# Attention and two feed-forward blocks on one core: GpSimd's arithmetic moved to VectorE, the first load split, the first scores turned round

## The chip, the cores and the metric

The kernel runs on one core of one Trainium2 chip. The metric is the device time of one execution in microseconds, the median over several runs. The engines are named as the profile names them: PE (TensorE, products and transposes), DVE (VectorE), ACT (ScalarE), POOL (GpSimd) and SP (SyncE, which here only issues DMAs).

## What is computed

The reference, cut to what matters; all of it is float32:

```python
scores = scale * np.matmul(q, k.transpose(0, 1, 3, 2))   # 2 batches, 12 heads, 448 x 64
scores = np.where(mask, -1000000000.0, scores)            # causal
scores = scores - np.max(scores, axis=-1, keepdims=True)
attn = np.exp(scores)
attn = attn / (np.sum(attn, axis=-1, keepdims=True) + 1e-09)
x = np.matmul(attn, v)                                    # -> 896 x 768
h = (x @ w1) * (x @ w2) @ w3 @ w_out                      # 768 -> 1024 -> 1024 -> 768
r = np.maximum(h @ w_in2, 0.0)                            # 768 -> 2048
out = (r * r) @ w_out2                                    # 2048 -> 768
```

## The kernel before

Everything is one stream of operations. A class `Program` (L28) collects them with what they read and write; `order` (L60) then lays them out by a list scheduler of its own, with a cost on each engine that may do the operation, and the kernel issues them in that order (L1287 to L1289), so the order on every engine is fixed when the program is built. Each operation is *due* when the PE step that needs it would start. An operation with two engines in its cost table goes where the planner finds it sooner: ACT or DVE for some copies, DVE or POOL for the scaling of the softmax (L688) and for subtractions whose operands all lie in SBUF (L446, L1029). POOL takes one of these if it would be done before DVE could begin it, or if it is due more than `SPARE` = 2500 ns later (L104). The flag `port` makes the planner keep a flagged operation of DVE or POOL from starting before the last flagged one of either has ended (L91).

The work runs in stages. *Attention* (to about 158 us in the profile): twelve pairs of heads. For a pair p, `load_pair` (L603) brings q and k, `scores` (L620) makes the scores of four row blocks of 112 (widths 448, 336, 224 and 112, because of the causal mask; `BLOCKS` at L600 gives the order, 448 first, and puts the last two in one PSUM bank), `minimum` (L660) adds the mask and takes each row's extreme on DVE, `softmax` (L666) takes the exponential with its sums on ACT, the reciprocal on DVE and the scaling of `p` on DVE or POOL (L689), `transposes` (L693) turns the scaled blocks on PE into `pp`, which ACT copies to `pt`, and `attend` (L714) makes `x`. The scores of pair p stand ahead of the transposes of pair p-1. After the scores of the second pair `warm` (L755) puts 36 transposes of the identity on PE. Between them PE multiplies `w3` and `w_out` (`w_half`, L558; tiles `w` and `wraw`), so that one weight replaces the two; their raw words go through `float32` (L482: L487 on ACT, L491 and L495 on DVE).

*First block* (158 to 320 us): products by Strassen's scheme in seven products (`product`, L1061; `h_step`, L1116). Every operand is split into a high part (rounded, ACT L440) and a low part (the rest, a DVE subtraction, L433), and three products of parts stand for one; `parts_of` (L442) adds these two operations. The weights' parts lie in `ring`, their sums in `xs`, other rows in `fs`. POOL adds the sums of the replaced weight by DMA (L821). *Second block* (from 320 us): the same for `w_in2`, then `g_out` (L1004), `need_block` (L1020) and `o_step` (L1208), whose sums go into `g` by DVE additions from PSUM (`g<-bank,g`).

One helper makes all subtractions, so they all stand at L433, all matrix products at L176, all copies at L440; the tiles tell them apart. What the change touches, with its callers:

Of the kernel before, what the change touches and what calls it, by code (L numbers as in the profile page):

```python
# [8 lines left out]
F32 = mybir.dt.float32  # L9
# [7 lines left out]
class Op:  # L17
# [4 lines left out]
    def __init__(self, place, engines, run, after, behind, port):  # L22
        self.place, self.engines, self.run, self.port = place, engines, run, port
        self.after, self.behind = after, behind
        self.due = self.start = self.end = None


class Program:  # L28
# [4 lines left out]
    SPARE = 2500  # L33
# [4 lines left out]
    def add(self, engines, run, reads=(), writes=(), port=False, after=(), behind=(), turn=None):  # L38
# [11 lines left out]
        op = Op(len(self.ops), engines, run, list(after), [o for o in behind if o not in after], port)  # L50
# [9 lines left out]
    def order(self):  # L60
# [18 lines left out]
        port, at_step = 0, 0  # L79
        avail = dict.fromkeys(ready, 0)  # L80
        while ready:
            best = None
            for e in clock:
# [6 lines left out]
                def begin(o):  # L90
                    held = port if e in "PV" and o.port else 0  # L91
                    return max(clock[e], avail[o], held)
# [5 lines left out]
                if e in "AP":  # L98
# [15 lines left out]
            if e in "PV" and o.port:  # L114
                port = t0 + gap
# [13 lines left out]
def attention_moe_moe2(ctx: ExitStack, tc: tile.TileContext, qk, v, w1, w2, w3, w_out, w_in2, w_out2, out):  # L129
# [21 lines left out]
    WARM = 36  # L151
# [186 lines left out]
    prog = Program({"S": 700})  # L338
    pools = {}
    engine_of = {"A": nc.scalar, "V": nc.vector, "P": nc.gpsimd}  # L340
# [8 lines left out]

    def pool(width):  # L350
        gap = 110 + 2.28 * width
        return {"P": (gap, gap + 30)}
# [89 lines left out]
    def parts_of(hi, lo, x, width, src, his, los, psum=False, any_engine=False, of=None):  # L442
# [39 lines left out]
    def float32(key, words, width, y, names):  # L482
# [16 lines left out]
        prog.add(dve(width, fast=True), lower, [low], [low], port=True)  # L499
        prog.add(dve(width), join, [low, *names], names, port=True)  # L500
# [14 lines left out]
    def w_row(key):  # L515
# [26 lines left out]
        prog.add(dve(width), tt(lo, y, lambda: hi_of(key).bitcast(F32), ALU.subtract), src + his, los, port=True)  # L542
# [60 lines left out]
    def load_pair(p):  # L603
# [4 lines left out]
        prog.add({"S": (1350, 3300)}, run, [], [("qk", p % 3)], turn="qk")  # L608
# [10 lines left out]

    def scores(p):  # L620
# [6 lines left out]
        for g in BLOCKS:  # L627
            for j in range(2):
                at[j, g] = turn("a", 6)
        for g in BLOCKS:  # L630
            o = 0
            for i in g:
                w = (i + 1) * CP

                def run(e, g=g, i=i, o=o, w=w):
                    if g == BLOCKS[0]:
# [8 lines left out]
                opened = [place_p(p, j, i2) for j in range(2) for i2 in range(NCH)] if g == BLOCKS[0] else []  # L645
                prog.add({"T": (1.856 * w, 1.856 * w + 250)}, run, [("qk", p % 3)],
                         [("a", at[j, g]) for j in range(2)] + opened)
                o += w
        for j in range(2):
            for g in BLOCKS:  # L650
# [15 lines left out]
    def softmax(p, j):  # L666
# [17 lines left out]
        for g in BLOCKS:  # L684
            for i in g:
                w = (i + 1) * CP
                on_v, on_p = 70 + 0.67 * w, 265 + 2.5 * w
                prog.add({"V": (on_v, on_v + 85), "P": (on_p, on_p + 30)},  # L688
                         lambda e, i=i: engine_of[e].tensor_scalar(  # L689
# [64 lines left out]

    def warm():  # L755
# [14 lines left out]

    for p in range(NP_ALL + 1):
# [64 lines left out]
    for k in range(KH):  # L836
        i, b = slot_in("T2", k), slot_in("B21", k)
        prog.add(dve(S), tt(fs_at(i), fs_at(b), fs_at(i), ALU.subtract), [("fs", i), ("fs", b)], [("fs", i)], port=True)
# [14 lines left out]
    def half_sum(out, x, z, what):  # L853
# [5 lines left out]
        prog.add(dve(HN), tt(half(out), half(x), half(z), what), [xs_half(*x), xs_half(*z)], [xs_half(*out)], port=True)  # L859
# [32 lines left out]
    def need_unit(u):  # L892
# [25 lines left out]
        else:  # L918
# [5 lines left out]
                 src + [("ring", i, "h") for i in slots], [("ring", i, "l") for i in slots], port=True)  # L924
# [19 lines left out]
    def ab_out(nm, m, b, n, i_bank):  # L944
# [12 lines left out]
        else:  # L957
            prog.add(dve(S), negated(row, fs_at(n), fs_at(a), ALU.mult), [("fs", n), ("fs", a)], names, port=True)
# [21 lines left out]
    def ab_sums(d):  # L980

        (r0, n0), (r1, n1), (r2, n2), (r3, n3) = (ab_row(d, i) for i in range(4))
        prog.add(dve(S), tt(r0, r0, r1, ALU.subtract), n0 + n1, n0, port=True)
        prog.add(dve(S), tt(r1, r3, r1, ALU.subtract), n1 + n3, n1, port=True)

        def t2():
            t = take_fs()
            prog.add(dve(S), negated(fs_at(t), r3, r0, ALU.subtract), n3 + n0, [("fs", t)], port=True)
            block_parts("ab", "T2", d, fs_at(t), ("fs", t))
            prog.add(dve(S), negated(r2, r2, fs_at(t), ALU.subtract), [*n2, ("fs", t)], n2, port=True)  # L990
# [13 lines left out]
    def g_out(nm, m, b, n, i):  # L1004
# [10 lines left out]
        parts_of(*part, lambda: fs[:, n, BN:], REST, ("fs", n), his, los, any_engine=True)  # L1015
# [4 lines left out]
    def need_block(g, n, d):  # L1020
# [7 lines left out]
        def sub(out, x, y):  # L1028
            prog.add(dve(BN) | pool(BN), tt(fs_at(out, BN), fs_at(x, BN), fs_at(y, BN), ALU.subtract),  # L1029
                     [("fs", x), ("fs", y)], [("fs", out)], port=True)  # L1030
# [6 lines left out]
        elif n == "7":  # L1037
# [3 lines left out]
                 his, los, any_engine=True)  # L1041
# [101 lines left out]
    def h_out(n, k, st, i):  # L1143
        o, src = bank_at(i), ("bank", i)

        def block(name, at):
            block_parts("h", name, k, fs_at(at), ("fs", at), any_engine=True)
# [4 lines left out]
        def sub(out, x, y):  # L1152
            prog.add(dve(S), tt(fs_at(out), fs_at(x), fs_at(y), ALU.subtract), [("fs", x), ("fs", y)], [("fs", out)],
# [184 lines left out]
```

## Time and profile before

| | us |
|---|---|
| median of 3 runs | 534.0 (533.85 to 537.04) |
| the profiled execution | 534.52 |
| its span on the core | 532.7 |
| PE busy | 519.2 |
| DVE busy | 492.3 |
| ACT busy | 383.9 |
| POOL busy | 103.2 |

The span runs from the core's first instruction to its last; the rest of the execution's time lies around it. Busy time is what an engine's instructions cover; those of DVE that follow each other overlap by some 0.08 us, so a row's mean is longer than the step from one to the next. PE's products are pipelined and their ends are modelled, so a busy PE may still be waiting a little.

### The profile page before, as it was taken

Reading aid. Unit: us, or ns where it says so; the run is one execution under the profiler, and the core shown is the slowest. Engines: PE = TensorE matmul, PEld = TensorE weight load, DVE = VectorE, ACT = ScalarE, POOL = GpSimd, SP = SyncE. Lnnn points to the kernel's source line nnn. Section 1 sums busy time; section 2 is a strip of 40 time slices with the busy share of each in tenths; the row PEclk is TensorE's granted clock in tenths of the full one; section 3 lists DMA queues with packets and bytes.
Section 4 is the critical chain, followed back from the end, with each engine's and each line's share of the span. In section 5 each row is a group of like instructions: output and inputs, shape, how many; then the busy total and the mean of one; then the engine's idle time right before and its main releaser. Section 6 shows DMA issues by size and latency. Waiting matters only on the chain.

```text
span 532.7 us, 8568 instructions
## 1 busy us (share of the span) xinstructions
PE 519.2 (97%) x2905; PEld 460.8 (86%) x2905; DVE 492.3 (92%) x1093; ACT 383.9 (72%) x890; POOL 103.2 (19%) x84
## 2 busy tenths in 40 slices
PE   7899999999999999999999999999999999999996
PEld 4658878888879999999999999999999989998985
DVE  5999898898999999997975899999999999999996
ACT  6998887777869565648475577986896489649950
POOL 2222211122110010221100034010115021505050
PEclk9999999999999999999999999999999999999999
DMA  8956554452642469999652402405430454035114
GB/s 317 322 166 220 169 180 148 147 170 61 249 156 83 177 184 252 260 254 248 153 163 93 172 0 73 165 1 201 155 120 0 148 178 150 0 132 175 51 59 149
DMA packets 26572, 81.30 MB, mean 153 GB/s; under 512 B 2400, under 2 KB 13408, under 8 KB 26528
## 3 DMA queue, kind: packets, MB, share of 16 engines
q1 hardware_dynamic: 22752, 75.24, 41.4%
q0 software_dynamic: 3776, 5.51, 6.4%
q8 instruction: 23, 0.38, 0.3%
q14 instruction: 21, 0.17, 0.1%
HBM read 74.84 MB, written 14.55 MB: 168 GB/s over the span
## 4 chain that ended last, share of the span: by engine, by line
PE 54%; DVE 21%; ACT 7%; DMA 2%; issue 2%; DVEq 0%
PE bank L176 43%; DVE g L433 6%; DVE ring L433 5%; PE w L176 5%; DVE xs L433 2%; DVE xs L495 2%; PE pp L704 2%; PE x L176 2%; DVE fs L433 2%; PE s L176 2%; ACT ring L440 1%; DMA raw_w<-in_w 1%; DMA raw_wout<-in_w_out 1%; ACT fs L1010 1%; ACT fs L1011 1%
## 5 line engine op out<-in xcount | busy, mean ns | idle before, releaser
L440 ACT CAST ring<-xs 128x384 fp32r<-128x384 f32 (+1 forms) x194 | 102.3, 542 | 59.2 <-DVE xs L433 21.4
L176 PE MATMUL bank<-xT,ring 128*128 128x448 f32 x630 | 132.2, 366 | 0.0
L433 DVE TENSOR_TENSOR ring<-xs,ring 128x384 fp32r<-128x384 f32 (+1 forms) x194 | 118.9, 631 | 12.2 <-ACT ring L440 12.0
L176 PEld LDWEIGHTS bank<-xT,ring 128*128 128x128 f32 x630 | 117.8, 188 | 9.6 <-ACT bank L440 0.5
L176 PE MATMUL bank<-ring,g 128*128 128x384 f32 x600 | 107.7, 337 | 3.0 <-DVE ring L433 2.0
L176 PEld LDWEIGHTS bank<-ring,g 128*128 128x128 f32 x600 | 103.8, 188 | 6.5 <-DVE ring L433 3.3
L176 PE MATMUL bank<-xB,ring 128*128 128x448 f32 x489 | 103.5, 367 | 0.7 <-ACT ring L440 0.4
L176 PEld LDWEIGHTS bank<-xB,ring 128*128 128x128 f32 x489 | 91.3, 188 | 10.0 <-ACT ring L440 1.4
L433 POOL TENSOR_TENSOR g<-fs,g 128x384 fp32r<-128x384 f32 (+1 forms) x24 | 37.2, 1562 | 127.7 <-ACT g L440 112.5
L672 ACT ACTIVATE p<-p,st 112x448 f32<-112x448 f32 (+3 forms) x96 | 49.9, 533 | 12.1 <-DVE st L662 12.1
L689 POOL TENSOR_SCALAR p<-p,st 112x224 f32<-112x224 f32 (+3 forms) x27 | 33.5, 1244 | 114.3 <-DVE st L681 62.4
L433 DVE TENSOR_TENSOR xs<-xs 128x384 f32<-128x384 f32 x96 | 54.4, 581 | 0.1
L662 DVE CUSTOM_DVE_ANT_0 p<-s,mask 112x224 f32<-112x224 f32 (+3 forms) x96 | 36.7, 440 | 6.4 <-PE s L176 6.3
L440 ACT CAST g<-fs 128x384 fp32r<-128x384 f32 (+1 forms) x88 | 34.4, 413 | 5.2 <-DVE fs L433 4.9
L176 PE MATMUL w<-hl_wout,w 128*128 128x384 f32 x192 | 36.2, 340 | 0.3 <-DVE wraw L433 0.2
L487 ACT ACTIVATE xs<-raw_w 128x768 f32<-128x768 f32 (+1 forms) x30 | 24.3, 814 | 14.7 <-DVE w L433 6.5
L176 PEld LDWEIGHTS w<-hl_wout,w 128*128 128x128 f32 x192 | 32.9, 188 | 1.9 <-issue 0.9
L821 POOL DMA_DIRECT2D s_dram<-w_dram x12 | 13.9, 1184 | 99.6 <-DMA s_dram<-w_dram 99.6
L176 PE MATMUL s<-qk 64*112 64x448 f32 (+3 forms) x192 | 28.2, 439 | 3.9 <-DMA qk<-in_qk 3.9
L433 DVE TENSOR_TENSOR g<-bank,g 128x384 f32<-128x384 f32 x60 | 30.1, 544 | 1.6 <-PE bank L176 1.6
L440 ACT COPY fs<-bank 128x448 f32<-128x448 f32 x49 | 25.8, 527 | 7.6 <-PE bank L176 7.6
L176 PE MATMUL bank<-ab,ring 128*128 128x448 f32 x144 | 29.5, 365 | 0.0
(82 smaller groups left out, 746.7 us busy)
## 6 DMA issues: line engine op xcount, KB each, us to landing
raw_wout<-in_w_out SPq DMA_DIRECT2D x24, 768.0 KB, 4.5
raw_w<-in_w SPq DMA_DIRECT2D x16, 768.0 KB, 4.5
raw_win<-in_w_in SPq DMA_DIRECT2D x16, 768.0 KB, 4.5
raw_w<-in_w SPq DMA_DIRECT2D x16, 512.0 KB, 4.1
qk<-in_qk SPq DMA_DIRECT2D x12, 448.0 KB, 5.7
s_dram<-w_dram POOLq DMA_DIRECT2D x8, 576.0 KB, 9.8
w_dram<-wraw SPq DMA_DIRECT2D x8, 384.0 KB, 2.9
s_dram<-w_dram SPq DMA_DIRECT2D x4, 768.0 KB, 7.1
```

The source lines that it names most:

```text
L176: return nc.tensor.matmul(o, l, r, start=start, stop=stop, **more)
L433: return lambda e: engine_of[e].tensor_tensor(out(), x(), y(), op=what)
L440: return lambda e: engine_of[e].copy(out(), x()) if e == "A" else engine_of[e].tensor_copy(out(), x())
L487: nc.scalar.activation(y(), raws[key][:, :, 1].bitcast(F32), AF.Prelu, scale=2.0 ** -112, alpha=-2.0 ** 32)
L495: nc.vector.scalar_tensor_tensor(yi, yi, 3, raws.pop(key)[:, :, 0], op0=ALU.logical_shift_left, op1=ALU.bitwise_or)
L662: prog.add({"V": (gap, gap + 160)}, lambda e: nc.vector.tensor_tensor_reduce(block(p, j, i), s_t[p, j, g][:CP, o:o + w], mask[:, S - w:], ...
L672: prog.add({"A": (gap, gap + 100)}, lambda e, i=i: nc.scalar.activation(block(p, j, i), block(p, j, i), AF.Exp, bias=st_t[p][:, 0, j, i:i ...
L689: lambda e, i=i: engine_of[e].tensor_scalar(block(p, j, i), block(p, j, i), st_t[p][:, 3, j, i:i + 1], None, ALU.mult),
L704: nc.tensor.transpose(x[0][:CP, o * CP:(o + 1) * CP], block(p, j, i)[:, c * CP:(c + 1) * CP], ident[:CP, :CP])
L821: prog.add({"P": (900, 5000)}, lambda e, x=x, n0=n0, n1=n1: nc.gpsimd.dma_start(out=s_dram[d][:, n0:n1], in_=spread(x, n1 - n0), accum_op= ...
L1010: prog.add(act(S, src[0] == "bank"), lambda e: nc.scalar.activation(r(), x(), AF.Relu), [src], [("fs", n)])
L1011: prog.add(act(S), lambda e: nc.scalar.activation(r(), r(), AF.Square), [("fs", n)], [("fs", n)])
```

## The change

Five edits, of which the first goes through the whole kernel.

1. POOL is left out of every cost table, and with it the `port` rule and `SPARE`: the 60 computing instructions that POOL had (27 scalings of `p`; 18 of `g` with 384 columns and 6 with 64; 8 of `fs`; 5 of `x` parts with 448 columns; in all of these but the scalings a subtraction) stand on DVE. POOL keeps the constants, the identity, the mask and the 12 DMAs that add. One copy to `wraw` goes from ACT to DVE by the planner's choice.
2. The first q and k tile comes in two DMAs of 224 columns each of q and k; the first two row blocks wait for the first only.
3. The first pair's blocks are taken from the narrowest on.
4. Ahead of them, five products of a 112x112 block of zeros, which DVE clears.
5. `warm` has 16 transposes instead of 36, and the planner prices the first pair's scores higher.

The diff, cut to its core:

```diff
-                if e in "AP":
+                if e == "A":
...
-                        return t0 + o.engines[e][0] < on_v or e == "P" and o.due > t0 + self.SPARE
+                        return t0 + o.engines[e][0] < on_v
...
-    WARM = 36
+    WARM = 16
+    WARM_UP = 5
...
-    prog = Program({"S": 700})
+    prog = Program({"S": 700, "V": 700})
...
-        engines = dve(width) | (pool(width) if any_engine else {})
-        prog.add(engines, tt(lo, x, lambda: hi().bitcast(F32), ALU.subtract), src + his, los, port=not psum)
+        prog.add(dve(width), tt(lo, x, lambda: hi().bitcast(F32), ALU.subtract), src + his, los)
...
+        def halves_of(n):
+            def run(e):
+                if n == 0:
+                    qk_t[p] = attq.tile([P, 2, S], F32, tag="qk", name=f"qk{p}", bufs=3)
+                own = slice(n * 2 * CP, (n + 1) * 2 * CP)
+                nc.sync.dma_start(
+                    out=qk_t[p][:, :, own], in_=qk[p].rearrange("p (i s) -> p i s", i=2)[:, :, own])
+
+            return run
+
+        if p == 0:
+            for n in range(2):
+                prog.add({"S": (675, 2400)}, halves_of(n), [], [("qk", p % 3, n)], turn="qk")
+            return
...
+        blocks = BLOCKS[::-1] if p == 0 else BLOCKS
...
-                prog.add({"T": (1.856 * w, 1.856 * w + 250)}, run, [("qk", p % 3)],
+                prog.add({"T": (cold(p, i) * w, cold(p, i) * w + 250)}, run, [("qk", p % 3, n) for n in range(1 + (i > 1))],
...
-                on_v, on_p = 70 + 0.67 * w, 265 + 2.5 * w
-                prog.add({"V": (on_v, on_v + 85), "P": (on_p, on_p + 30)},
+                on_v = 70 + 0.67 * w
+                prog.add({"V": (on_v, on_v + 85)},
...
+    def warm_up():
+        place = turn("w", 2)
+        prog.add({"V": (200, 300)}, lambda e: nc.vector.memset(xs[:CP, 0, :CP], 0.0), [], [("xs", 0, 0)])
+
+        def run(e):
+            t, x = ps_w.tile([P, HN], F32, tag="w", name="warm_up"), xs[:CP, 0, :CP]
+            for _ in range(WARM_UP):
+                mm(t[:CP, :CP], x, x, True, True)
...
-            prog.add(dve(BN) | pool(BN), tt(fs_at(out, BN), fs_at(x, BN), fs_at(y, BN), ALU.subtract),
-                     [("fs", x), ("fs", y)], [("fs", out)], port=True)
+            prog.add(dve(BN), tt(fs_at(out, BN), fs_at(x, BN), fs_at(y, BN), ALU.subtract),
+                     [("fs", x), ("fs", y)], [("fs", out)])
```

How the instructions stand. The last number of a name is that of its buffer. In a score's name the first number is the head of the pair and the second the block (3 is the one of 448 columns; 0 stands for the bank that blocks 0 and 1 share). PE at the start of the program, before:

```order
L176 MATMUL s_0_3_123<-qk_114 112x448
L176 MATMUL s_1_3_125<-qk_114 112x448
L176 MATMUL s_0_2_129<-qk_114 112x336
L176 MATMUL s_1_2_131<-qk_114 112x336
L176 MATMUL s_0_0_134<-qk_114 112x112
L176 MATMUL s_1_0_136<-qk_114 112x112
L176 MATMUL s_0_0_134<-qk_114 112x224
L176 MATMUL s_1_0_136<-qk_114 112x224
```

and after the change:

```order
L173 MATMUL warm_up<-xs 112x112 x5
L173 MATMUL s_0_0_129<-qk_115 112x112
L173 MATMUL s_1_0_131<-qk_115 112x112
L173 MATMUL s_0_0_129<-qk_115 112x224
L173 MATMUL s_1_0_131<-qk_115 112x224
L173 MATMUL s_0_2_139<-qk_115 112x336
L173 MATMUL s_1_2_141<-qk_115 112x336
L173 MATMUL s_0_3_147<-qk_115 112x448
L173 MATMUL s_1_3_149<-qk_115 112x448
```

The products of zeros stand first, and the order of the blocks is turned round.

DVE where the first pair's softmax ends (`p_121` and `p_122` are its two heads, `st_120` its sums; L662 is the minimum of the second pair), before:

```order
L662 ISA p_146,st_145<-s_0_2_156,mask 112x336
L662 ISA st_145 112x1
L689 TENSOR_SCALAR p_121<-p_121,st_120 112x448
L689 TENSOR_SCALAR p_121<-p_121,st_120 112x336
L689 TENSOR_SCALAR p_121<-p_121,st_120 112x112
L680 TENSOR_SCALAR st_120<-st_120 112x4
L681 RECIPROCAL st_120<-st_120 112x4
L662 ISA p_147,st_145<-s_1_2_158,mask 112x336
L662 ISA st_145 112x1
```

with POOL's first scalings, which stand behind its mask:

```order
L332 AFFINE_SELECT mask<-mask 112x448
L689 TENSOR_SCALAR p_121<-p_121,st_120 112x224
L689 TENSOR_SCALAR p_122<-p_122,st_120 112x224
L689 TENSOR_SCALAR p_146<-p_146,st_145 112x224
L689 TENSOR_SCALAR p_146<-p_146,st_145 112x112
```

DVE after the change, where `p_127` and `p_128` are the first pair's heads and L699 is the scaling:

```order
L699 TENSOR_SCALAR p_127<-p_127,st_126 112x448
L699 TENSOR_SCALAR p_127<-p_127,st_126 112x336
L699 TENSOR_SCALAR p_127<-p_127,st_126 112x224
L699 TENSOR_SCALAR p_127<-p_127,st_126 112x112
L690 TENSOR_SCALAR st_126<-st_126 112x4
L691 RECIPROCAL st_126<-st_126 112x4
L672 ISA p_160,st_158<-s_1_2_170,mask 112x336
L672 ISA st_158 112x1
L699 TENSOR_SCALAR p_128<-p_128,st_126 112x448
L699 TENSOR_SCALAR p_128<-p_128,st_126 112x336
L699 TENSOR_SCALAR p_128<-p_128,st_126 112x224
L699 TENSOR_SCALAR p_128<-p_128,st_126 112x112
```

POOL's two scalings of 224 columns now stand among DVE's, one for each head.

The end of the second block, POOL before (the last of its instructions):

```order
L433 TENSOR_TENSOR g_3578<-fs,g_3578 128x384
L433 TENSOR_TENSOR fs<-fs 128x384
L433 TENSOR_TENSOR g_3406<-fs,g_3406 128x384
L433 TENSOR_TENSOR g_3578<-fs,g_3578 128x384 x2
L433 TENSOR_TENSOR g_3406<-fs,g_3406 128x384 x2
L433 TENSOR_TENSOR fs<-fs 128x384 x2
L433 TENSOR_TENSOR g_3371<-fs,g_3371 128x384
```

DVE after the change, in the same part of the program (L426 is the helper's subtraction or addition):

```order
L426 TENSOR_TENSOR ring<-xs,ring 128x384
L426 TENSOR_TENSOR g_3569<-fs,g_3569 128x384
L426 TENSOR_TENSOR g_3537<-bank_1948,g_3537 128x384
L426 TENSOR_TENSOR g_3537<-bank_2186,g_3537 128x384
L426 TENSOR_TENSOR ring<-xs,ring 128x384
L426 TENSOR_TENSOR g_3569<-fs,g_3569 128x384
L426 TENSOR_TENSOR xs<-xs 128x384
L426 TENSOR_TENSOR fs<-fs 128x384
L426 TENSOR_TENSOR xs<-xs 128x384
L426 TENSOR_TENSOR g_3537<-bank_1946,g_3537 128x384
L426 TENSOR_TENSOR ring<-xs,ring 128x384
L426 TENSOR_TENSOR g_3284<-fs,g_3284 128x384
```

The `fs<-fs` and `g<-fs,g` subtractions stand between the parts of the weights (`ring<-xs,ring`) and the additions from PSUM (`g<-bank,g`), all on one engine.

## Rows read from the trace of the kernel before

**Rows 1.** The page, busy time of each engine, its share of the span and instructions.
```profile
PE 519.2 (97%) x2905; PEld 460.8 (86%) x2905; DVE 492.3 (92%) x1093; ACT 383.9 (72%) x890; POOL 103.2 (19%) x84
```

**Rows 2.** Windows by stage: length, then PE, PEld, DVE, ACT, POOL, clock, DMA.
```profile
0.00:27.00 27.00, 21.76 (x149) 15.37 (x150) 20.50 (x78) 20.72 (x57) 6.40 (x13) 1.00 0.90 319
27.00:160.00 133.00, 132.25 (x889) 104.87 (x888) 123.49 (x367) 105.56 (x292) 28.74 (x22) 1.00 0.50 167
160.00:320.00 160.00, 160.00 (x791) 148.14 (x791) 142.59 (x252) 102.92 (x197) 19.63 (x17) 1.00 0.61 169
320.00:388.00 68.00, 67.97 (x358) 64.46 (x357) 66.14 (x130) 55.92 (x125) 12.12 (x8) 1.00 0.35 120
388.00:524.00 136.00, 132.30 (x699) 123.31 (x698) 135.63 (x263) 98.28 (x223) 36.30 (x24) 1.00 0.29 98
```

**Rows 3.** Waits of PE, 388 to 524 us: total, times, longest.
```profile
PE bank L176 <- DVE ring L433: 2.0, 3, 0.7
```

**Rows 4.** Chain that ended last, in order of time, one piece: start, length.
```profile
398.83 1.87 DVE g L433 x4
```

**Rows 5.** Timeline of PE, 0 to 28 us: start, length, instruction, idle before.
```profile
3.90 6.69 PE L176 MATMUL s<-qk 64*112 64x448 f32 x32 [3.90 <-DMA qk<-in_qk]
10.53 3.66 PE L761 MATMUL warm<-ident 112*112 112x112 f32 x36
14.03 2.08 PE L704 MATMUL pp<-ident,p 112*112 112x112 f32 x20
16.04 2.22 PE L176 MATMUL x<-pt,v 112*64 112x448 f32 x16
18.18 2.15 PE L176 MATMUL s<-qk 64*112 64x448 f32 x16
20.66 2.85 PE L176 MATMUL w<-xs,w 128*128 128x384 f32 x8 [0.33 <-DVE w L495]
...
25.83 1.29 PE L704 MATMUL pp<-ident,p 112*112 112x112 f32 x10 [0.92 <-DVE p L689]
```

**Rows 6.** POOL by line and shape, 388 to 524 us: busy, mean ns, idle.
```profile
L433 POOL TENSOR_TENSOR g<-fs,g 128x384 fp32r<-128x384 f32 x15 | 23.2, 1559 | 63.0 <-ACT g L440 47.8 <-DVE g L433 15.2
L433 POOL TENSOR_TENSOR fs<-fs 128x384 f32<-128x384 f32 x7 | 10.1, 1446 | 18.4 <-DVE fs L433 18.4
```

**Rows 7.** Timeline of DVE around 499 us.
```profile
499.10 0.22 DVE L433 TENSOR_TENSOR g<-fs,g 128x64 fp32r<-128x64 f32 x1
499.23 0.55 DVE L433 TENSOR_TENSOR xs<-xs 128x384 f32<-128x384 f32 x1
```

**Rows 8.** DVE by line and shape, 388 to 524 us.
```profile
L433 DVE TENSOR_TENSOR ring<-xs,ring 128x384 fp32r<-128x384 f32 x74 | 44.4, 624 | 0.0
L433 DVE TENSOR_TENSOR xs<-xs 128x384 f32<-128x384 f32 x39 | 24.1, 630 | 0.0
L433 DVE TENSOR_TENSOR g<-bank,g 128x384 f32<-128x384 f32 x48 | 24.0, 543 | 0.0
...
L433 DVE TENSOR_TENSOR fs<-fs 128x384 f32<-128x384 f32 x17 | 10.9, 644 | 0.0
...
L433 DVE TENSOR_TENSOR g<-fs,g 128x64 fp32r<-128x64 f32 x19 | 4.8, 261 | 0.2
```

**Rows 9.** DVE by line and shape, 160 to 240 us.
```profile
L433 DVE TENSOR_TENSOR ring<-xs,ring 128x384 fp32r<-128x384 f32 x42 | 22.6, 548 | 0.9 <-ACT ring L440 0.9
```

**Rows 10.** Timeline of DVE, around 520 us.
```profile
520.10 1.08 DVE L433 TENSOR_TENSOR ring<-xs,ring 128x384 fp32r<-128x384 f32 x1
```

**Rows 11.** Timeline of all engines, 0 to 16 us.
```profile
0.74 0.86 SPq L606 DMA_DIRECT2D qk<-in_qk  x2
...
5.89 0.62 DVE L662 CUSTOM_DVE_ANT_0 p<-s,mask 112x448 f32<-112x448 f32 x1 [5.89 <-PE s L176]
...
9.49 0.62 DVE L662 CUSTOM_DVE_ANT_0 p<-s,mask 112x448 f32<-112x448 f32 x1 [0.38 <-PE s L176]
...
11.28 1.16 DVE L689 TENSOR_SCALAR p<-p,st 112x448 f32<-112x448 f32 x3
```

More of the change, by code (lines that the diff above doesn't have):

```diff
@@ L17, with __init__ @@
 class Op:
-    def __init__(self, place, engines, run, after, behind, port):
-        self.place, self.engines, self.run, self.port = place, engines, run, port
+    def __init__(self, place, engines, run, after, behind):
+        self.place, self.engines, self.run = place, engines, run
         self.after, self.behind = after, behind
@@ L32, with add @@
     HOP = 80
-    SPARE = 2500
     def __init__(self, clock):
         self.ops, self.wrote, self.read, self.clock, self.turns = [], {}, {}, clock, {}
-    def add(self, engines, run, reads=(), writes=(), port=False, after=(), behind=(), turn=None):
+    def add(self, engines, run, reads=(), writes=(), after=(), behind=(), turn=None):
         after, behind = dict.fromkeys(after), dict.fromkeys(behind)
@@ L49, in add @@
             behind[self.turns[turn]] = None
-        op = Op(len(self.ops), engines, run, list(after), [o for o in behind if o not in after], port)
+        op = Op(len(self.ops), engines, run, list(after), [o for o in behind if o not in after])
         if turn:
@@ L606, in run @@
             nc.sync.dma_start(out=t.rearrange("p i s -> p (i s)"), in_=qk[p])
-        prog.add({"S": (1350, 3300)}, run, [], [("qk", p % 3)], turn="qk")
+        def halves_of(n):
[10 more added lines that the diff above has]
+            return
+        prog.add({"S": (1350, 3300)}, run, [], [("qk", p % 3, n) for n in range(2)], turn="qk")
     def load_v(p):
@@ L626, in scores @@
         at = {}
-        for g in BLOCKS:
+        blocks = BLOCKS[::-1] if p == 0 else BLOCKS
+        for g in blocks:
             for j in range(2):
                 at[j, g] = turn("a", 6)
-        for g in BLOCKS:
+        for g in blocks:
             o = 0
@@ L635, in run @@
                 def run(e, g=g, i=i, o=o, w=w):
-                    if g == BLOCKS[0]:
+                    if i == blocks[0][0]:
                         open_tiles()
@@ L643, in run @@
                         mm(s_t[p, j, g][:CP, o:o + w], y[own, 0, i * CP:(i + 1) * CP], y[own, 1, :w], True, True)
[L645 to L646 removed]
+                opened = [place_p(p, j, i2) for j in range(2) for i2 in range(NCH)] if i == blocks[0][0] else []
+                prog.add({"T": (cold(p, i) * w, cold(p, i) * w + 250)}, run, [("qk", p % 3, n) for n in range(1 + (i > 1))],
                          [("a", at[j, g]) for j in range(2)] + opened)
@@ L649, in scores @@
         for j in range(2):
-            for g in BLOCKS:
+            for g in blocks:
                 o = 0
@@ L857, in half @@
             return lambda: in_slot(of[0])[:, of[1] * HN:(of[1] + 1) * HN]
-        prog.add(dve(HN), tt(half(out), half(x), half(z), what), [xs_half(*x), xs_half(*z)], [xs_half(*out)], port=True)
+        prog.add(dve(HN), tt(half(out), half(x), half(z), what), [xs_half(*x), xs_half(*z)], [xs_half(*out)])
     def need_item(it):
@@ L923, in need_unit @@
         prog.add(dve(width), tt(lambda: t[1], x, lambda: t[0].bitcast(F32), ALU.subtract),
-                 src + [("ring", i, "h") for i in slots], [("ring", i, "l") for i in slots], port=True)
+                 src + [("ring", i, "h") for i in slots], [("ring", i, "l") for i in slots])
     def ring_names(u):
```

51 lines of the change are left out of this document (24 added, 27 removed).

## Prediction

> **What bounds the kernel now.** I read the busy line first, then the windows by stage, then the waits of PE and the chain that ended last in the stage that the windows single out. The busy line [rows 1] has PE at 519.2 us and DVE at 492.3 us of 532.7 us: two engines near full, and their average hides that they bind in different places. The windows [rows 2] part them. From 27 to 388 us PE is busy 360.2 of 361 us (132.25, 160.00 and 67.97) and DVE has gaps: 9.5 us before 160, 17.4 us from there to 320, 1.9 us from 320 to 388. From 388 to 524 us it is the other way: DVE is busy 135.63 of 136 us and PE is idle for 3.7 us, 2.0 of them for parts of weights that DVE makes [rows 3]. In that stage the chain runs over DVE in steps of 0.47 us, as in the row of four additions in 1.87 us [rows 4]. Before 27 us PE waits longest: 3.90 us for the first q and k, then for DVE, 0.33 us before `w` at 20.66 and 0.92 us before `pp` at 25.83 [rows 5]. So a change to DVE's work counts in full in two places, the first 26 us and the last 136 us, and nearly nothing between.
>
> **The change, part by part.** *GpSimd's work goes to DVE, last stage.* POOL has 24 instructions there [rows 2], 22 of them of 128x384 [rows 6] and 2 of 128x64. On DVE a 128x384 step is 0.467 us (1.87/4) [rows 4]; a 128x64 step is 0.13 us, from 499.10 to the next start at 499.23 [rows 7]. Added: 22 x 0.467 + 2 x 0.13 = 10.5 us. What goes is what POOL costs DVE. The same DVE instructions are longer in this stage than between 160 and 240 us, where POOL computes nothing: `ring<-xs,ring` 624 against 548 ns, x74, is 5.6 us; against the same 548 for the same columns, `xs<-xs` at 630, x39, is 3.2 us and `fs<-fs` at 644, x17, 1.6 us; the 128x64 one, 261 ns against the 0.22 us of a single one at 499.10, x19, is 0.8 us [rows 7 to 9]. Together 11.2 us. That it is POOL is seen from what is not stretched: `g<-bank,g`, one of whose inputs is in PSUM, means 543 ns in the stage where its SBUF neighbours take 624 [rows 8]. So DVE's balance is 10.5 - 11.2 = -0.7 us. Bounds: +10.5 us if the stretch stays although POOL is quiet, and -3.7 us, all of PE's idle time there, if the relief falls just where PE waits, as at 520.10, where a `ring` step of 1.08 us, stretched, is one of those that PE waits for [rows 3, 10]. I take -0.7, since rows give both terms.
>
> *The same, from 27 to 388 us.* The 22 scalings of `p` that POOL does between 27 and 160 us cost DVE at most 0.47 us each, the step of 384 columns [rows 4] (most have 224), 10.3 us, and one more `wraw` copy that ACT loses 0.47 us. DVE's 9.5 us of gaps in that stage [rows 2] take them, but for 1.3 us at that bound. Five `x` parts of 448 columns go into the 17.4 us before 320; the eight before 388, four of 128x384 and four of 128x64 (1.9 + 0.5 us), go into 1.9 us of gaps, and what those eight take from DVE now goes as well. So the cost is bounded by 1.3 + 0.5 us, what the gaps can't hold, and the gain by PE's 0.8 us of idle time. I take 0. Nothing waits longer: an instruction on DVE is 0.5 us where POOL needs 1.45 to 1.56 us [rows 6].
>
> *First load in two parts, narrow blocks first.* Now PE starts at 3.90, 3.16 us after the issue of the whole tile of 448 KB at 0.74; DVE's first minimum starts at 5.89, because 2 x 448 columns come first, and ACT's first exponential comes after it [rows 5, 11]. Half of the bytes at the stage's 319 GB/s [rows 2] are 0.7 us less, so 3.2 us; the bounds are that and 3.9 (no gain). The first minimum then waits for 112 and 224 columns of both heads, 336 instead of 448: 1.99 us x 336/448 = 1.5 us, so it starts at 4.7, 1.2 us earlier (bounds 5.4 and, if PE already runs twice as fast, 3.9). DVE's pause of 0.38 us before the second pair [rows 11] may shrink, or an equal one may open before the 336 block if the second part is late; I leave them against each other. From there to 26 us DVE is the one waited for, and the lead carries. POOL's five scalings of this stage stand on it too, 5 x 0.47 = 2.3 us at most; by the balance of the last stage, where a POOL instruction costs DVE as much as doing it, nearly 0. I take 0.2, so the start gives -1.0 us (bounds -2.0 and +1.5). The split adds one DMA issue, half of the 0.86 us that two take on SP [rows 11], in front of the second q and k, `v` and the weights; PE first uses the weights at 20.66 [rows 5], so for them this is covered, and the second pair's scores come behind the first's anyway.
>
> *Products of zeros, 16 transposes instead of 36.* The five products need only a small memset by DVE, idle until 5.89, and end before the load. The 36 transposes end at 14.19, though head 0's three DVE scalings are done at 12.44 [rows 5, 11]. With 16 (16 x 3.66/36 = 1.6 us) PE reaches `pp` some 2 us earlier; but `w` at 20.66 waits for DVE and not for `pp`, so this is worth nothing by itself. [...]
>
> [...]
>
> *Sum.* -0.7 + 0 - 1.0 = -1.7 us. Against the profiled execution (534.5 us, a span of 532.7 and 1.8 around it) that is 532.8; that execution lies 0.5 us above the median of 534.0, so the forecast for a median is 532.3 us.
>
> **Rivals.** *DVE, alone, becomes dearer than POOL was.* If only half of the 11.2 us of stretch goes, the last stage gets 10.5 - 5.6 = 4.9 us longer, because DVE has no gap there to take it: 534.0 - 1.0 + 4.9 = 537.9 us. It decides for slower as soon as less than 9.5 us of the stretch goes (10.5 less the 1.0 of the start). For it: DVE at 135.63 of 136 us. Against it: the mean of 548 ns without POOL, and the unstretched PSUM shapes.
> *The relief hits the waits.* PE's 3.7 us of idle time in the last stage go as well, because what was late there were stretched `ring` parts, and POOL's results no longer come after 1.5 us: 534.0 - 1.0 - 3.7 = 529.3 us. Against it: DVE's total hardly falls, and DVE is full.
> [...]
>
> **How the numbers follow.** Chances: the forecast 0.48; nothing from the start 0.20; relief that hits the waits 0.17; DVE dearer 0.15. A measurement of this kernel can tell about 1% (5.3 us) from no change. The forecast's own range is 530.5 to 534.5. The wide one goes down to 528.9 (the relief, and 0.4 of the further 1.0 us that the start's bound allows) and up to 537.0, most of the way to the dearer DVE. Faster by over 1% means under 528.7: only the relief together with the best start gets there, 0.12. Slower by over 1%, over 539.3, needs the dearer DVE at more than half: 0.09. The rest is 0.79.
>
> **What would show it.** Right: POOL's busy time falls to its constants and 12 DMA issues; DVE's `ring<-xs,ring` means about 548 ns also after 388 us; DVE is still full there, with a busy sum within 2 us of 135.6; the first minimum starts near 4.7 us and `pp` of the second pair near 24.8. Wrong: `ring` steps that still mean over 580 ns; gaps of DVE after 388 us, waiting for ACT or PE; a first score later than 3.6 us; score products or `pp` at twice their steps after 12 us; or PE waits of more than 1 us between 27 and 388 us, which would mean that the gaps of DVE were no cover.

## The result, and the profile after

The changed kernel takes 529.7 us (median of 5 runs, 529.48 to 530.95); the kernel before, on the same chip, 534.6. The ratio is 0.990, with an interval of 0.986 to 0.993: a gain of 0.7 to 1.4%, on the edge of what can be told from no change. The forecast was 532.3 us with a range of 528.9 to 537.0. The number lies in the range, 2.6 us under the forecast, and the steps behind it hold less well than the number does. The profiled execution took 529.48 us with a span of 527.7, against 534.52 and 532.7 before, so 5.0 us are to be placed.

The page's busy line, after:

```profile
PE 516.0 (98%) x2895; PEld 460.5 (87%) x2895; DVE 491.3 (93%) x1159; ACT 385.4 (73%) x889; POOL 15.0 (3%) x20
```

POOL's count fell from 84 to 20 [rows 1], so the change moved 64 computing instructions (27 + 18 + 6 + 8 + 5), not the 60 given with it. DVE has 66 more: those, the clearing of the zeros and the copy to `wraw`.

Windows by stage, after (length, then PE, PEld, DVE, ACT, POOL, clock, DMA):

```profile
0.00:27.00 27.00, 22.21 (x133) 14.55 (x134) 20.48 (x80) 21.83 (x57) 1.62 (x8) 1.00 0.91 312
27.00:160.00 133.00, 133.00 (x905) 107.06 (x904) 125.90 (x398) 106.84 (x294) 0.00 (x0) 1.00 0.51 170
...
388.00:524.00 136.00, 132.96 (x716) 126.35 (x714) 135.20 (x289) 96.69 (x216) 0.00 (x0) 1.00 0.31 102
```

Waits of PE from 388 to 524 us, after; this is the whole answer:

```profile
PE bank L173 <- DVE g L426: 1.4, 3, 0.7
```

DVE by line and shape, 388 to 524 us, after:

```profile
L426 DVE TENSOR_TENSOR ring<-xs,ring 128x384 fp32r<-128x384 f32 x72 | 38.2, 551 | 0.0
L426 DVE TENSOR_TENSOR g<-bank,g 128x384 f32<-128x384 f32 x54 | 28.2, 549 | 0.0
L426 DVE TENSOR_TENSOR g<-fs,g 128x384 fp32r<-128x384 f32 x40 | 22.0, 551 | 0.0
L426 DVE TENSOR_TENSOR xs<-xs 128x384 f32<-128x384 f32 x39 | 21.0, 551 | 0.0
L426 DVE TENSOR_TENSOR fs<-fs 128x384 f32<-128x384 f32 x23 | 12.7, 551 | 0.0
...
L426 DVE TENSOR_TENSOR g<-fs,g 128x64 fp32r<-128x64 f32 x21 | 4.4, 219 | 0.0
```

All 128x384 shapes now have one length. `ring<-xs,ring` fell from 624 to 551 ns, `xs<-xs` from 630, `fs<-fs` from 644, while `g<-bank,g`, which reads PSUM, stayed (543 and 549) [rows 8]. DVE does 26 instructions more in this window and is as full as before; the 2.0 us that PE waited for `ring` [rows 3] are gone.

The busy line alone would mislead: PE's busy time fell by 3.2 us, though behind the start PE does the same products, and at the start the 20 transposes fewer (3.66 us for 36, 1.75 for 16) are made up for by the products of zeros (2.21 us). Part of a wait is drawn as PE busy time, as the attention shows below.

To place the 5.0 us I laid the starts of the same PE products of two traces side by side; the table gives start minus start in the kernel before, in us (negative is earlier), the median over the products of a stretch. It stands here for all runs of this study.

| kernel | 28 to 60 us | 100 to 145 | 165 to 240 | 388 to 400 | span |
|---|---|---|---|---|---|
| changed | +0.55 | -1.6 | -2.1 | -2.05 | -5.0 |
| changed, e11 | +0.25 | -1.9 | -2.4 | -2.2 | -4.7 |
| e1 edit 1 alone | -0.2 | -2.3 | -2.8 | -3.3 | -6.4 |
| e12 edit 1 alone | -0.05 | -2.15 | -2.2 | -2.65 | -5.8 |
| e2 start edits alone | 0.0 | -0.6 to -0.2 | +0.3 | +0.3 | +1.7 |
| e3 scalings on DVE | -0.1 | -2.2 | -2.1 | -2.1 | +0.4 |
| e4 subtractions on DVE | -0.1 | -0.3 | -0.6 | -0.65 | -3.3 |
| e5 load whole | 0.0 | -2.1 | -2.6 | -2.7 | -5.1 |
| e6 no zeros | +0.4 | -1.7 | -2.2 | -2.7 | -5.9 |
| e7 products of 0.37 | +0.3 | -1.8 | -2.3 | -2.8 | -5.2 |
| e8 old start, WARM 16 | +0.1 | -2.0 | -2.5 | -3.0 | -4.8 |
| e9 more POOL, last stage | -0.4 | -2.5 | -2.9 | +0.2 | +6.3 |
| e10 more POOL, attention | 0.0 | -1.3 | -1.7 | -2.0 | -4.7 |

So the changed kernel loses 0.55 us at the start (forecast: gains 1.0), gains 2.6 us between 60 and 165 us (forecast: 0), nothing to 388, and 2.95 us in the last stage (forecast: 0.7). The span of one execution is uncertain by about 1 us: e3's profiled execution took 534.9 us, its median is 533.7.

**The start.** PE, after:

```profile
1.04 2.21 PE L173 MATMUL warm_up<-xs 112*112 112x112 f32 x10 [1.04 <-DVE xs L767]
3.87 7.18 PE L173 MATMUL s<-qk 64*112 64x112 f32 x32 [0.62 <-DMA qk<-in_qk]
...
15.94 2.11 PE L173 MATMUL x<-pt,v 112*64 112x448 f32 x16
19.36 2.15 PE L173 MATMUL s<-qk 64*112 64x448 f32 x16 [1.32 <-DMA qk<-in_qk]
21.82 2.85 PE L173 MATMUL w<-xs,w 128*128 128x384 f32 x8 [0.30 <-DVE w L487]
```

The half load let PE start at 3.87 us; the whole one did so at 3.90 [rows 5]. The second half landed at 4.82 us, so the whole pair was there 0.96 us later than with one load (3.86). SP's issues and DVE's first minima, after:

```profile
0.74 1.34 SPq L605 DMA_DIRECT2D qk<-in_qk  x2
2.12 0.59 SPq L598 DMA_DIRECT2D qk<-in_qk  x1
```
```profile
5.49 0.39 DVE L672 CUSTOM_DVE_ANT_0 p<-s,mask 112x224 f32<-112x224 f32 x1 [4.51 <-PE s L173]
...
7.98 0.62 DVE L672 CUSTOM_DVE_ANT_0 p<-s,mask 112x448 f32<-112x448 f32 x1 [0.54 <-PE s L173]
...
9.67 0.62 DVE L672 CUSTOM_DVE_ANT_0 p<-s,mask 112x448 f32<-112x448 f32 x1 [0.51 <-PE s L173]
```

Two half loads keep SP for 1.34 us, where the whole tile and the next whole tile together took 0.86 [rows 11]. The second pair's q and k landed at 7.70 us (5.67 before), the four `raw_wout` at 11.64 to 17.44 (10.02 to 15.66), the third q and k at 19.23 (17.45). For this last one PE now waits 1.32 us, a wait that the trace of before does not have. DVE's first minimum came 0.40 us earlier, not 1.2, and DVE then paused twice for more than half a microsecond. The lead was spent by 10 us.

**The attention.** PE and its weight loads (PEld) at the same place, before:

```profile
77.53 2.91 PE L704 MATMUL pp<-ident,p 112*112 112x112 f32 x20
```
```profile
77.53 0.38 PEld L704 LDWEIGHTS pp<-ident,p 112*112 112x112 f32 x4 [0.38 <-DVE st L662]
78.07 1.64 PEld L704 LDWEIGHTS pp<-ident,p 112*112 112x112 f32 x13 [0.17 <-DVE st L662]
79.94 0.28 PEld L704 LDWEIGHTS pp<-ident,p 112*112 112x112 f32 x3 [0.22 <-DVE st L662]
```

and after:

```profile
77.52 2.08 PE L714 MATMUL pp<-ident,p 112*112 112x112 f32 x20
```
```profile
77.35 2.03 PEld L714 LDWEIGHTS pp<-ident,p 112*112 112x112 f32 x20
```

Before, PE shows no idle time here, only 20 transposes that take 2.91 us where 2.08 are usual; the row of the weight loads tells why, they waited three times for DVE's minima. DVE began those minima at 76.85 us, after the change at 74.78. The lag against the kernel before steps at six places between 66 and 150 us, which carry the 2.6 us; this one and the product just ahead of it make 1.4 of them. What PE waited for at the others was not followed.

**The last stage.** One wait of the kernel before, on DVE and POOL:

```profile
409.96 1.37 POOL L433 TENSOR_TENSOR g<-fs,g 128x384 fp32r<-128x384 f32 x1 [0.96 <-ACT g L440]
410.38 1.37 DVE L433 TENSOR_TENSOR fs<-fs 128x384 f32<-128x384 f32 x1
411.67 1.48 DVE L433 TENSOR_TENSOR ring<-xs,ring 128x384 fp32r<-128x384 f32 x3
...
412.74 1.49 PE L176 MATMUL bank<-ring,g 128*128 128x384 f32 x7 [0.68 <-DVE ring L433]
```

The `fs<-fs` that starts 0.42 us after POOL's instruction is held until that one has ended (411.33 us) and takes 1.37 us instead of 0.55, and the `ring` parts behind it are late for PE. After the change the same product has no wait. At the very end it turned round: before, DVE's last three additions waited for PE; after, six follow each other without a pause.

```profile
527.94 1.60 DVE L433 TENSOR_TENSOR g<-bank,g 128x384 f32<-128x384 f32 x3 [1.63 <-PE bank L176]
```
```profile
520.33 2.87 DVE L426 TENSOR_TENSOR g<-bank,g 128x384 f32<-128x384 f32 x6
```

DVE ends at 523.20 us instead of 529.55, 6.35 us earlier, and 1.35 us of that are given back, most of it by the stores: the last output store is now issued at 524.35, behind stores that SP issues 0.5 us apart, slower than DVE's 0.467, where before it was issued at 529.57, as soon as DVE was done.

### The profile page after: what moved, and what is told of

Same layout as the page of the kernel before. It is cut to its first block, busy times and chain, and to the rows that moved or that the text cites. A ratio compares the mean times of both kernels' runs of the same rounds, so it can differ in the third digit from the quotient of the medians.

```text
span 527.7 us, 8441 instructions
## 1 busy us (share of the span) xinstructions
PE 516.0 (98%) x2895; PEld 460.5 (87%) x2895; DVE 491.3 (93%) x1159; ACT 385.4 (73%) x889; POOL 15.0 (3%) x20
## 4 chain that ended last, share of the span: by engine, by line
PE 63%; DVE 26%; ACT 7%; issue 2%; DMA 2%; DVEq 0%
PE bank L173 37%; PE w L173 13%; DVE g L426 7%; DVE ring L426 6%; PE s L173 5%; PE x L173 4%; DVE fs L426 4%; PE pp L714 4%; DVE xs L426 3%; DVE xs L487 2%; ACT ring L433 2%; ACT xs L479 1%; DMA raw_wout<-in_w_out 1%; ACT fs L1033 1%; DVE xB L426 1%
## 5 line engine op out<-in xcount | busy, mean ns | idle before, releaser
L426 DVE TENSOR_TENSOR ring<-xs,ring 128x384 fp32r<-128x384 f32 (+1 forms) x194 | 111.4, 588 | 12.2 <-ACT ring L433 12.0
L173 PE MATMUL bank<-ring,g 128*128 128x384 f32 x600 | 105.9, 335 | 1.4 <-DVE g L426 1.4
L682 ACT ACTIVATE p<-p,st 112x224 f32<-112x224 f32 (+3 forms) x96 | 50.0, 530 | 9.7 <-DVE st L672 9.7
L426 DVE TENSOR_TENSOR xs<-xs 128x384 f32<-128x384 f32 x96 | 51.7, 552 | 0.1
L433 ACT CAST g<-fs 128x384 fp32r<-128x384 f32 (+1 forms) x88 | 35.5, 423 | 14.9 <-DVE fs L426 14.7
L426 DVE TENSOR_TENSOR g<-fs,g 128x384 fp32r<-128x384 f32 (+1 forms) x88 | 36.8, 430 | 0.2 <-ACT g L433 0.2
L426 DVE TENSOR_TENSOR g<-bank,g 128x384 f32<-128x384 f32 x60 | 31.4, 549 | 0.0
L173 PE MATMUL s<-qk 64*112 64x112 f32 (+3 forms) x192 | 28.7, 443 | 1.9 <-DMA qk<-in_qk 1.9
L699 DVE TENSOR_SCALAR p<-p,st 112x448 f32<-112x448 f32 (+1 forms) x96 | 29.1, 359 | 0.1
L173 PEld LDWEIGHTS bank<-ab,ring 128*128 128x128 f32 x144 | 27.0, 188 | 2.1
```

What stands on the lines that cost most here:

```text
L173: return nc.tensor.matmul(o, l, r, start=start, stop=stop, **more)
L426: return lambda e: engine_of[e].tensor_tensor(out(), x(), y(), op=what)
L433: return lambda e: engine_of[e].copy(out(), x()) if e == "A" else engine_of[e].tensor_copy(out(), x())
L682: prog.add({"A": (gap, gap + 100)}, lambda e, i=i: nc.scalar.activation(block(p, j, i), block(p, j, i), AF.Exp, bias=st_t[p][:, 0, j, i:i ...
L699: lambda e, i=i: nc.vector.tensor_scalar(block(p, j, i), block(p, j, i), st_t[p][:, 3, j, i:i + 1], None, ALU.mult),
```

## The experiments

Theory 1: the whole gain is edit 1 (POOL computes nothing), and the edits to the start cost half a microsecond. Theory 2: the start carries part of it. Expectations are quoted as written before each run; "before" is the kernel before, on the same chip.

**e1, edit 1 alone.** The changed kernel with the old start:

```diff
-        if p == 0:
-            for n in range(2):
-                prog.add({"S": (675, 2400)}, halves_of(n), [], [("qk", p % 3, n)], turn="qk")
-            return
...
-        blocks = BLOCKS[::-1] if p == 0 else BLOCKS
+        blocks = BLOCKS
...
-    WARM = 16
+    WARM = 36
...
-    warm_up()
```

> Edit 1 alone: GpSimd computes nothing, the first load whole, the widest block first, no products of zeros, WARM 36 as before. Theory 1 (the whole gain is GpSimd's removal, the edits to the start cost about 0.55 us): 529.0 us, 5.5 us under before and about 0.5 us under the changed kernel; the first score at 3.9 us, the second round of scores at 18.2 us as before, the first product of the first layer 2.5 us earlier than before. Theory 2 (the edits to the start carry part of the gain): 531 to 533 us, above the changed kernel.

528.76 us, ratio 0.987 (0.984 to 0.989). Theory 1 holds. It is the lowest ratio of all versions, though its interval overlaps those of the others with edit 1.

**e2, edits 2 to 5 alone**, POOL keeping its work: the start's functions of the changed kernel put into the kernel before.

> Edits 2 to 5 alone: the first load in two parts, the narrowest block first, products of zeros, the new planner prices at the start; GpSimd keeps its work. Theory 1: 535.0 us, 0.5 us over before, the second round of scores about 1.2 us later than before and the lag still 0.5 us at 60 us. Theory 2: 531 to 533 us, under before.

536.18 us, ratio 1.001 (0.999 to 1.003): no gain. With e1 that rules theory 2 out. Not all of theory 1's detail came: at 60 us it was level, not 0.5 us late.

**e3 and e4, edit 1 in two halves.** In the kernel before, only the scalings (e3) or only the subtractions (e4) lose POOL:

```diff
-                on_v, on_p = 70 + 0.67 * w, 265 + 2.5 * w
-                prog.add({"V": (on_v, on_v + 85), "P": (on_p, on_p + 30)},
+                on_v = 70 + 0.67 * w
+                prog.add({"V": (on_v, on_v + 85)},
```
```diff
-        engines = dve(width) | (pool(width) if any_engine else {})
+        engines = dve(width)
...
-            prog.add(dve(BN) | pool(BN), tt(fs_at(out, BN), fs_at(x, BN), fs_at(y, BN), ALU.subtract),
+            prog.add(dve(BN), tt(fs_at(out, BN), fs_at(x, BN), fs_at(y, BN), ALU.subtract),
```

> Before, with only the scalings of p taken from GpSimd (20 instructions); its subtractions of the last stage stay. Theory 1 (VectorE and GpSimd hold each other up, or GpSimd's slow scalings end late in the attention): the gain of 2.6 us between 60 and 158 us of the trace comes back and the last stage stays: 532.0 us. Rival (the attention's gain came from the new order of the start): 534.6 us, as before.

> Before, with only the subtractions of the last stage taken from GpSimd (22 instructions); its scalings stay. Theory 1: the last stage gains about 2.9 us and VectorE's ring subtractions there fall from 624 to about 588 ns: 531.6 us. Rival (my forecast's sum: VectorE gets as much work as it loses in stretch): 533.9 us.

e3: 533.69 us, ratio 0.997 (0.995 to 0.999), 1.8 us under before. e4: 530.95 us, 0.991 (0.988 to 0.994), 4.5 us under. Together 6.3, against e1's 6.7, so the halves add up. (The edits take all 27 scalings and all 37 subtractions from POOL, more than the 20 and 22 that the expectations name.) The table puts each in its stage: e3 has 2.0 us of the attention's gain (2.1 to 2.6 in the versions with the whole of edit 1 and nothing added), e4 2.65 of the last stage's 2.95. `ring` from 388 to 524 us in e3 and in e4:

```profile
L433 DVE TENSOR_TENSOR ring<-xs,ring 128x384 fp32r<-128x384 f32 x74 | 44.1, 620 | 0.0
```
```profile
L433 DVE TENSOR_TENSOR ring<-xs,ring 128x384 fp32r<-128x384 f32 x73 | 38.6, 549 | 0.0
```

The stretch goes with POOL's subtractions, to 549 ns and not to the 588 that I had written down, which is the page's mean over all shapes of the line.

**e5, e6, e8: parts of the start**, each on the changed kernel: the load whole (e5, the first four minus lines of e1's diff); no `warm_up()` (e6); old start but WARM 16 (e8). The score products run at two rates at the start: in the trace of before the two products of one 448-column block take 0.75 us from start to start at 4.79 us and 0.38 us at 18.65. The expectations speak of these two as levels and as the clock; the granted clock reads 1.00 beside both.

> The changed kernel with the first load of q and k whole, as before; narrowest block first and zeros stay. Theory 1 (the split delays every later transfer by 1.6 to 2 us and brings the first half no earlier): the first score at 3.9 us as in the changed kernel, the third load of q and k at about 17.5 us, TensorE's wait of 1.3 us for it gone, 0.5 to 1.2 us faster than the changed kernel, 528.5 to 529.2 us. Rival (the split costs nothing, the delay is the order of the start): as the changed kernel, 529.7 us.

> The changed kernel without the products of zeros ahead of the first scores. Theory 1 (products of zeros do not bring the clock up): scores at the low level until about 9.9 us as with them, 529.7 us. Rival (they bring the clock up sooner): the low level lasts about 2 us longer and the kernel takes 0.5 to 1 us more.

> Edit 1 with WARM 16 only: whole load, widest block first, no zeros. Against e1 (WARM 36) this shows what the number of fillers is worth. Theory 1: within 0.3 us of e1, 529.0 us. Rival (fewer fillers cost clock at the start): 529.5 to 530.5 us.

529.84 (e5), 529.27 (e6) and 528.78 us (e8), with ratios of 0.989, 0.989 and 0.988, all within 0.003 either way: the times can't rank them, and the 0.5 to 1.2 us that e5 was expected to gain don't show. The traces tell a little more. In e5 the third q and k landed at 17.39 us and PE's wait for them is gone, as expected. But the landing scatters by itself: with the first load whole (9 traces) it came between 17.23 and 18.84 us, on average at 17.8, and late ones make PE wait too (1.71 us in e8); with the split (5 traces) always between 18.75 and 19.23. So the split costs this load 1.2 us on average. Of the kernels with edit 1, those with a whole load (e1, e5, e8, e9, e10, e12) stand at -0.4 to +0.1 at 28 to 60 us, the four with the split (changed, e6, e7, e11) at +0.25 to +0.55: some 0.45 us between their means. e2, split and level, doesn't fit, and this stays open.

**e7, products that are not zero and leave no gap:**

```diff
-        prog.add({"V": (200, 300)}, lambda e: nc.vector.memset(xs[:CP, 0, :CP], 0.0), [], [("xs", 0, 0)])
+        prog.add({"V": (200, 300)}, lambda e: nc.vector.memset(xs[:CP, 0, :CP], 0.37), [], [("xs", 0, 0)])
...
-    WARM_UP = 5
+    WARM_UP = 9
```

> The changed kernel with 18 products of a constant 0.37 instead of 10 of zeros, so that no gap stands between them and the scores. If the data (zero) or the gap of 0.6 us kept the clock low: the scores' low level ends before 9 us and the kernel gains 0.3 to 1 us. If neither: low level until about 9.9 us, and the scores start later by whatever the products run past the load's landing at 3.8 us (0 to 0.5 us lost).

529.51 us, 0.989 (0.986 to 0.991). The score products reached their upper rate (the start of the first two products of a block that take under 1.0 ns a column, where the 0.75 us of before are 1.67 and the 0.38 us are 0.84; the granted clock reads 1.00 in every window of the start) at 6.9 us, though they began 0.8 us late, more than expected. But kernels with nothing at all ahead of the scores reached it at 6.7 (e9), 7.0 (e8), 7.5 (e1), 9.3 (before) and 10.2 us (e6), and with the zeros it was 7.7 (e2), 8.9 (e5), 9.2 (e11) and 10.0 us (changed). The scatter of 3.5 us covers every difference: the zeros show no effect, and for 0.37 one run decides nothing. Two rows, of e9 and of e6, both without products ahead:

```profile
3.81 5.91 PE L173 MATMUL s<-qk 64*112 64x448 f32 x32 [3.81 <-DMA qk<-in_qk]
```
```profile
3.95 7.01 PE L173 MATMUL s<-qk 64*112 64x112 f32 x32 [3.95 <-DMA qk<-in_qk]
```

**e9, POOL's disturbance put back, its work not.** In e1's kernel, 24 subtractions on POOL that read an `fs` row and a scratch row:

```diff
...
+        if n in "147":
+            prog.add({"P": (1100, 1130)}, lambda e: nc.gpsimd.tensor_tensor(
+                extra[:, :BN], fs_at(row, BN)(), extra[:, :BN], op=ALU.subtract), [("fs", row)], [("extra",)])
```

> The kernel of e1 (VectorE does all) with 24 subtractions added on GpSimd in the last stage, each of an activation row and a scratch row, 128x384, whose result nobody reads: VectorE's and TensorE's work is that of e1. Theory 1 (VectorE's instructions with two SBUF inputs run longer while GpSimd works): ring and xs subtractions beside them take about 800 to 870 ns instead of 551, some 12 us of stretch over 24, and 535 to 541 us against e1's 528.8. Rival (the gain of the last stage came from the order, not from contention): VectorE's durations and the time as e1.

541.13 us, ratio 1.012 (1.009 to 1.016), 11.9 over e12 on the same chip, with no work added to DVE or PE. PE, DVE and ACT run the same instructions in the same order in the traces of e9 and e12, so the rival (order) falls. PE's waits for DVE's `g` from 388 to 524 us went from 1.4 us to

```profile
PE bank L173 <- DVE g L428: 4.0, 5, 1.2
```

Since the order is the same, the two traces can be laid side by side instruction by instruction. From 300 us on DVE's steps, from start to start, are 11.8 us longer in e9: 23 instructions are longer by 0.2 to 0.83 us each, and every one of them overlaps one of POOL's 24. One of them, with POOL's:

```profile
459.50 1.20 POOL L1062 TENSOR_TENSOR extra<-fs,extra 128x384 f32<-128x384 f32 x1 [19.98 <-ACT ring L435]
460.19 0.91 DVE L428 TENSOR_TENSOR ring<-xs,ring 128x384 fp32r<-128x384 f32 x1
```

So the expected 12 us came. They sit in few instructions, most of them longer than the expected 800 to 870 ns, and `ring` means only 580 ns because most of the 70 in that window are not lengthened. DVE's own waits grew by 1.0 us, nearly all of it one wait of 1.12 us for ACT at 483.82 us, and ACT had waited for PE: after waits of 0.32, 0.95 and 1.20 us for `g`, PE took 3.85 us for 12 products from 474.48 us on (12 steps of 0.17 us, the median of the products of 384 columns in the trace of before from 388 to 524 us, are 2.1 us), and the granted clock reads 0.58 from 474 to 476 us and 0.56 from there to 478 (0.99 over the whole of 388 to 524 us, where the kernel before and the changed one read 1.00). No other trace here has such a fall between its start and its end, and why it fell, no run shows. Stretch and waits together are DVE's whole delay, which leaves next to nothing for activation rows that POOL held longer.

Some of POOL's instructions were kept out, too:

```profile
372.41 12.52 POOL L1062 TENSOR_TENSOR extra<-fs,extra 128x384 f32<-128x384 f32 x2 [11.80 <-ACT fs L1030]
```

For the first 10 of these 12.5 us DVE ran `ring`, `xs`, `g<-fs` and parts of raw words back to back at their usual steps (0.47 us for 384 columns): 20 instructions that started after POOL's ran ahead of it, and POOL got through only when a `fs<-bank` came, at 382.67 us. So in e9 each engine held the other up: POOL by these 10 us, DVE by 0.2 to 0.83 us in each of the 23 instructions.

**e10, the same for the attention.** In e1's kernel, 27 scalings on POOL into a scratch row:

```diff
...
+                if p and j == 1 and (i > 1 or i == 1 and p % 2 == 0):
+                    prog.add({"P": (265 + 2.5 * w, 295 + 2.5 * w)}, lambda e, i=i, w=w: nc.gpsimd.tensor_scalar(
+                        extra[:CP, :w], block(p, j, i), 0.5, None, ALU.mult), [place_p(p, j, i)], [("extra",)])
```

> The kernel of e1 with 27 scalings added on GpSimd in the attention, whose results go to a scratch row that nobody reads. Theory 1 (contention cost the attention its 2.1 us): scalings of p on VectorE beside them take 550 instead of 390 to 450 ns, and 530 to 531 us. Rival (the gain came because results of GpSimd no longer arrive late and the minima come first): 528.8 us as e1, with VectorE's longer scalings in its idle time.

530.58 us, 0.992 (0.989 to 0.994), 1.4 us over e12. Against e12's trace 0.9 of the attention's 2.15 us are lost again at 100 to 145 us and 0.45 at 165 to 240, with POOL busy for 41.9 us there (28.7 before). So POOL's scalings cost the attention something even where nobody waits for their results. How much of the gain that explains is open, since e10 put back less than half of the disturbance: by their means and counts from 27 to 160 us, DVE's scalings of `p` are 2.6 us longer than in e12 (224 columns: 436 ns, not the expected 550, against 331), in the kernel before 6.4 us. The order differs, too. In the kernel before `hl_wout`, 0.87 us, stands just ahead of the minima of the place above; in e10, which has the order of e12, it stands behind them, DVE begins them at 75.42 us, between e12's 74.60 and the 76.85 of before, and the weight loads of `pp` don't wait:

```profile
76.83 2.03 PEld L715 LDWEIGHTS pp<-ident,p 112*112 112x112 f32 x20
```

No run shows what the order alone would have brought.

**e11 and e12, the changed kernel and e1 once more, on one chip.**

> The changed kernel once more, beside the next on one chip. Theory 1: 529.7 us. If the edits to the start cost nothing, as the next.

> Edit 1 alone once more, as the version that may beat both kernels: 528.8 us, 0.5 to 1.4 us under the changed kernel if the edits to the start cost what the traces show; level with it if their cost lies within what a run varies by.

529.78 us (0.9900, 0.9875 to 0.9925) and 529.20 us (0.9891, 0.9867 to 0.9916). Edit 1 alone was the faster both times, by 0.6 us here; the intervals overlap, so that it beats the changed kernel is likely and not proven. Against the kernel before it gains 1.3% (e1) and 1.1% (e12).

## Why the prediction was right or wrong

*GpSimd's work goes to DVE, last stage: mechanism right, term mis-sized.* A gain of 0.7 us was forecast, 2.95 us came. I took -11.2 us of stretch and +10.5 us of work. By the steps from start to start, from the same product (388.0 before, 385.95 after) to DVE's end, the stretch that went is 12.3 us (`ring` 6.1, `xs` 3.3, `fs` 1.6, 128x64 1.1, the rest 0.2), the work 9.7, and DVE's own waits, which the sum left out, 1.8, nearly all the 1.63 us at the end: together DVE is done in 4.4 us less. A window that stopped at 524 us couldn't show that wait. Then 1.35 us went back behind DVE's end, mostly to the stores. e4 and e9 show the cause: the stretch goes when POOL's subtractions go, and 11.8 us of it return with 24 subtractions whose result nobody reads.

What ran longer beside POOL are DVE's instructions whose inputs lie in SBUF: `ring` took 624 ns with POOL's subtractions and 551 without, while `g<-bank,g`, with one input in PSUM, took 543 and 549. The one held up was not always the one that started second: the `fs<-fs` at 410.38 us was held by a POOL instruction that had started 0.42 us earlier, but in e9's 12.5 us row 20 of DVE's instructions started after POOL's and still ran ahead of it.

*27 to 388 us: wrong.* The step that failed is "the gain [is bounded] by PE's 0.8 us of idle time". PE gained 2.6 us there, because waits are drawn as longer products: at 77.53 us, where PE's row has no idle time, the weight loads waited for 0.38, 0.17 and 0.22 us, and their rows showed it in the trace of before. Nothing became dearer: DVE's idle time did cover the moved work, as forecast, though only 10 of the 22 scalings, not most, have 224 columns and ten are wider. e3 shows that the gain comes with the scalings; how it divides between contention and order stays open.

*The start: wrong.* A gain of 1.0 us was forecast; the two traces of the changed kernel are 0.55 and 0.25 us late. "Half of the bytes ... are 0.7 us less, so 3.2 us" failed: the first half landed at 3.83 us, the whole tile at 3.86. So the time to landing was not set by its bytes here. The bounds of 3.9 us for the first minimum and of -2.0 us for the start counted on PE running twice as fast for the first scores, and no run shows that: the rate did double (0.75 to 0.38 us for a block of 448 columns in the trace of before), but at 6.7 us at the earliest and 10.2 at the latest, after the first scores. "The lead carries" failed too; "covered" failed for the second issue, since everything behind it landed 1.6 to 2 us later in this pair of traces (1.2 us for the third q and k over all runs) and PE waited 1.32 us for that load, which I hadn't followed. That nothing comes from the start, which had a chance of 0.20, is what came, and the half load that lands no earlier is one reason; why it does, no run shows. The 16 transposes in place of 36 cost PE no rate: the first 10 `pp` behind them stand 0.096 us from start to start but for one step of 0.144, where the kernel before has 0.096 too, and took 1.17 us where 20 take 2.08.

*The rivals.* "The relief hits the waits" named 529.3 us and the mechanism of the last stage; it came within 0.4 us, but with 2.95 instead of 3.7 us there, and the missing start was made up by the attention. That is luck. "DVE dearer" fell: the whole stretch went.

*The number.* 1.7 us of gain were forecast and 5.0 us came in the traces. The three stages missed by +1.55 (start), -2.6 (27 to 388 us) and -2.25 us (last stage); that the first has the other sign brought the sum nearer by luck, and the low end of the range was that of a rival. Of the signs named, `ring` at 551 ns, DVE's 135.2 us and POOL's 15.0 us came; the first minimum (5.49 us, not 4.7), the second pair's `pp` (26.50, not 24.8) and the first score (3.87, later than 3.6) spoke against the start.

## What to carry to other kernels

Before giving a little work to GpSimd, compare the mean of VectorE's instructions whose inputs lie in SBUF with that of the same shape where GpSimd is quiet (`ring` here: 624 and 548 ns): in this kernel each GpSimd instruction cost VectorE 0.51 us (12.3 us over 24; 11.8 over 24 in e9), more than the 0.467 us of doing the work itself. A gain is not bounded by the idle time of the PE row (0.8 us of it from 27 to 388 us here, and 2.6 us of gain); look at the waits of the weight loads and at products that run longer than their kind. Splitting a load buys nothing where the first half lands no earlier, as here (3.83 and 3.86 us), and the transfers behind it can pay for the extra issue (1.2 us for the third q and k): follow the queue to the last load that someone waits for.

## What the runs showed that I had not expected

A DMA of half a tile took SP 0.69 us to issue where the whole one took 0.39, and landed at the same time (3.83 and 3.86 us). Later loads of one and the same queue landed up to 1.6 us apart from run to run (the third q and k). TensorE's products reached their upper rate at times from 6.7 to 10.2 us, whatever ran ahead of them. And GpSimd was kept waiting by VectorE for 10 us (e9, from 372.41 us on), inside a row that reads as busy.
